# Weight decoding one VectorE operation at a time, and half products for the first batch too

## The chip, the cores and the metric

The kernel runs on one core of a Trainium2 chip. The time of an execution is the device time of that core in microseconds. A profile shows the engines PE (TensorE, the matmuls; PEld is its loading of weights), DVE (VectorE), ACT (ScalarE), POOL (GpSimd) and SP (SyncE, which issues nearly all transfers here). Each engine works through its own queue in program order and waits where an operand or a buffer is not ready.

## The reference

Routed attention with 4 batches, 8 heads, 768 tokens and 64 elements to a head, and after it a feed-forward block on the joined heads.

```python
q_assign = np.argmax(np.einsum('bhsd,hcd->bhsc', q_n, c_n), axis=-1)   # 16 clusters
k_assign = np.argmax(np.einsum('bhsd,hcd->bhsc', k_n, c_n), axis=-1)
mask = q_assign[:, :, :, None] == k_assign[:, :, None, :]
scores = np.where(mask, scale * np.matmul(q, k.transpose(0, 1, 3, 2)), -1e9)
attn = np.exp(scores - np.max(scores, axis=-1, keepdims=True))
attn = attn / (np.sum(attn, axis=-1, keepdims=True) + 1e-09)
x = np.matmul(attn, v)            # joined to 3072 tokens x 512
h = x @ w_in                      # 512 x 2048
g = h * np.clip(h + 3.0, 0.0, 6.0) / 6.0
return (g @ w_out)                # 2048 x 512
```

q, k, v and the result are float32. `w_in` and `w_out` reach the kernel as float64, that is as pairs of 32-bit words, and the kernel builds float32 weights from the two words.

## The kernel before

The attention runs over 16 pairs of heads (4 pairs to a batch), and a pair takes 12 steps: 2 halves of the 384 queries times 6 blocks of 128 keys. The main loop takes two steps at a time, so I call one pass a double step. `n` counts steps (0 to 190, by twos), and `r = n % 12` says where in the pair it is. Batch 0 is n = 0 to 46, batch 1 is n = 48 to 94.

The program is written out by hand in the order in which each engine is to run it (`tc.manual_schedule()`). One double step issues, in this order:

1. `scores` for two steps: PE multiplies q and k (L354), ACT takes the exponential `ex` (L366), and POOL adds the exponentials up in `acc` (L370 and L373; ten additions a pair, none where a half begins; `ex` has four buffers).
2. `attn_v` for the two steps before: PE (L383), and at the end of a half an ACT copy `num` (L389).
3. `in_range`, two ACT passes over the reciprocal of the divide before (L416, L417), and twice in a pair (r = 2 and r = 8) `divide`: PE sums `acc` into `pd` (L404), DVE takes the reciprocal `rcp` (L408) and multiplies it into `xT` (L409).
4. the preparation of the next pair, one part at a time: `turn` (r = 0 and 2), `cluster_scores` (r = 4, PE L291), `route` (r = 6, PE L302 and then DVE `mx` and `one_hot`, L305 and L311), `route_turn` (r = 8 and 10, PE L334).
5. some items of the feed-forward block, as many as `items_by(n + 2)` says.
6. in chosen double steps (`slots`) the decoding of one chunk of weights.

The small PSUM tiles of the parts 3 and 4 come from `scratch`. While `st["early"]` holds (up to `DECODED`), one in three of them is a buffer of its own (`psum_t`, one buffer) and two in three come from `psum_m` (two buffers), which the feed-forward block uses too. So the fourth scratch tile waits for the first, in effect: `route_turn` at r = 10 and `cluster_scores` at r = 4 each wait for the `rcp` of the double step before to have read `pd`.

There are 32 chunks of weights (16 of `w_in`, 16 of `w_out`, 128 x 512 each). `decode_weights(i)` is two ACT passes (L210, L213) and five DVE operations one behind the other: L219, L223, L226, L230 and L233. `load_weights(i + 1)` goes ahead of it; the raw words have two buffers, so that a load waits until the chunk two before has been read. The slots are r = 0, 4, 10 in batch 0 (12 chunks) and r = 0, 2, 4, 6, 10 in batch 1 (20 chunks), the last at n = 94; `DECODED` is 96.

The feed-forward block of batch 0 (`ffn_items`) takes 384 tokens at a time: 16 `up` items (four matmuls of 384 columns, L440, then the gate: ACT L427, DVE L428) and 12 `down` parts (four matmuls of 512 columns, L457), twice. Its first 16 `up` items are spread over n = 52 to 94, and the other 40 items fall to n = 96 to 102. The batches 1 to 3 use `fast_items`: 256 tokens at a time, 8 `up` items (eight matmuls of 256 columns, L504, and after every second one four DVE operations on the gated values, L516) and 7 `down` parts of eight matmuls of 256 columns (L522). The seven parts take the place of eight half-size products: sums and differences of blocks are formed first, as in Strassen's scheme. They need the weight sums `T1` to `T4`, which `weight_sums` forms in eight DVE operations (L493), one in each double step from n = 96.

After the loop's last attention step whatever is left of the feed-forward block runs alone.

Of the kernel before, what the change touches and what calls it, by code (L numbers as in the profile page):

```python
# [8 lines left out]
F32 = mybir.dt.float32  # L9
BF16 = mybir.dt.bfloat16  # L10
U32 = mybir.dt.uint32
I32 = mybir.dt.int32
ALU = mybir.AluOpType
ACT = mybir.ActivationFunctionType
# [4 lines left out]
P = 128  # L19
NCH = S // P  # L20
NC2 = 2 * NCH
HALF = S // 2
NHC = NCH // 2
NG = B * H
NPAIR = NG // 2
DM = 512
DFF = 2048
NKT = DM // P
NFT = DFF // P
WC = 512  # L30
NW = NKT * DFF // WC + NFT
# [85 lines left out]
def fast_path(ctx, tc, ok, q, k, v, centroids, moe_w_in, moe_w_out, out):  # L117
# [3 lines left out]
    nc = tc.nc  # L121
# [15 lines left out]
    yp = pool("yp", 1)  # L137
    decoding = ctx.enter_context(ExitStack())
    rawp = decoding.enter_context(tc.tile_pool(name="rawp", bufs=2))
    decp = decoding.enter_context(tc.tile_pool(name="decp", bufs=2))  # L140
# [3 lines left out]
    psum_m = pool("psum_m", 2, space=PSUM)  # L144
# [54 lines left out]
    def load_weights(i):  # L199
        if i < len(chunks):  # L200
            st["raw", i] = rawp.tile([P, WC, 2], U32, name="raw")
            nc.sync.dma_start(st["raw", i], chunks[i][1])

    def decode_weights(i):
        if not 0 <= i < len(chunks):
            return
        dst, raw = chunks[i][0], st.pop(("raw", i))
        lo, hi = raw[:, :, 0], raw[:, :, 1]
        size = decp.tile([P, WC], BF16, name="wsize")
        nc.scalar.activation(  # L210
            out=size, in_=hi.bitcast(F32), func=ACT.Abs, accum_out=w_totals[:, 0, i : i + 1]
        )
        nc.scalar.activation(  # L213
            out=size, in_=size, func=ACT.Relu, bias=w_low, scale=-1.0,
            accum_out=w_totals[:, 1, i : i + 1],
        )
        top = decp.tile([P, WC], U32, name="wtop")
        unit = decp.tile([P, WC], U32, name="wunit")
        nc.vector.tensor_scalar(  # L219
            out=top, in0=hi, scalar1=3, scalar2=0x3FFFFFFF,  # L220
            op0=ALU.logical_shift_left, op1=ALU.bitwise_and,
        )
        nc.vector.scalar_tensor_tensor(  # L223
            out=top, in0=hi, scalar=0xC0000000, in1=top, op0=ALU.bitwise_and, op1=ALU.bitwise_or
        )
        nc.vector.tensor_scalar(  # L226
            out=unit, in0=top, scalar1=0xFF800000, scalar2=None, op0=ALU.bitwise_and
        )
        top, unit = top.bitcast(F32), unit.bitcast(F32)
        nc.vector.scalar_tensor_tensor(  # L230
            out=unit, in0=lo, scalar=2.0**-52, in1=unit, op0=ALU.mult, op1=ALU.mult
        )
        nc.vector.tensor_tensor(out=dst, in0=top, in1=unit, op=ALU.add)  # L233

# [188 lines left out]
    def gate(g, h):  # L425

        nc.scalar.activation(out=g, in_=h, func=ACT.Relu, bias=half_c, scale=1.0 / 6.0)  # L427
        nc.vector.scalar_tensor_tensor(out=g, in0=g, scalar=1.0, in1=h, op0=ALU.min, op1=ALU.mult)  # L428


    def ffn_items(b):
        slots = g_sb.rearrange("p k i c -> p (k i c)")

        def up(hf, f):
            def item():
                xT = st["xT", b]
                ph = psum_m.tile([P, 512], F32, name="ph", tag="m")
                hh = ph[:, 0:HALF]
                for kt in range(NKT):
                    nc.tensor.matmul(  # L440
                        hh, lhsT=w_in_sb[:, kt, f * P : (f + 1) * P],
                        rhs=xT[:, kt, hf * HALF : (hf + 1) * HALF],
                        start=(kt == 0), stop=(kt == NKT - 1),
                    )
                at = (hf * NFT + f) % 18 * HALF
                st["g", f] = slots[:, at : at + HALF]
                gate(st["g", f], hh)

            return item

        def down(hf, i, part):
            def item():
                if part == 0:
                    st["y"] = psum_m.tile([P, DM], F32, name="py", tag="m")
                py = st["y"]
                for f in range(part * 4, part * 4 + 4):
                    nc.tensor.matmul(  # L457
                        py, lhsT=st["g", f][:, i * P : (i + 1) * P], rhs=w_out_sb[:, f],
                        start=(f == 0), stop=(f == NFT - 1),
                    )  # L460
                if part == 3:
                    y = yp.tile([P, DM], F32, name="y", tag=f"y{i % 2}")
                    nc.vector.tensor_copy(out=y, in_=py)
                    nc.sync.dma_start(out_v[b, hf * NHC + i], y)

            return item

        items = []
        for hf in range(2):
            items += [up(hf, f) for f in range(NFT)]  # L470
            items += [down(hf, i, part) for i in range(NHC) for part in range(4)]
        return items

# [3 lines left out]
    def weight_sums(i):  # L481
        if i == 0:
            decoding.close()
            wtp = pool("wtp", 1)
            for name in ("T1", "T2", "T4"):
                st[name] = wtp.tile([P, HF, HC], F32, name=name)
            st["T3"] = wb[0][1]
        name, a, b = (
            ("T1", wb[0][1], wb[0][0]), ("T2", wb[1][1], st["T1"]), ("T4", wb[1][0], st.get("T2")),
            ("T3", wb[1][1], wb[0][1]),  # L490
        )[i // 2]
        h = slice(i % 2 * HF // 2, (i % 2 + 1) * HF // 2)
        nc.vector.tensor_tensor(out=st[name][:, h], in0=a[:, h], in1=b[:, h], op=ALU.subtract)  # L493


    def fast_items(b):
        def up(m, i):
            def item():
                xT = st["xT", b]
# [72 lines left out]
    def prep_items(g, r):  # L572
# [13 lines left out]
    per_batch = NKT * per_pair  # L586
    total = NPAIR * per_pair
    lag_v, lag_d = 2, 4
    up_half = NFT
    per_ffn = 2 * (NFT + NHC * 4)  # L590
    per_fast = NHC * (HF + 7)

    slots = [
        n for n in range(0, total, 2)
        if n % per_pair in ((0, 4, 10) if n < per_batch else (0, 2, 4, 6, 10))
    ][:NW]
    READY, DECODED = per_batch + lag_d, slots[-1] + 2

    END = 2 * per_batch + NCH + 2

    def items_by(n):

        if n <= DECODED:
            return max(n - READY, 0) * up_half // (DECODED - READY)
        if n <= END:
            return up_half + (n - DECODED) * (per_ffn - up_half) // (END - DECODED)
        return per_ffn + (n - END) * per_fast // per_batch

    st["early"] = True
    fill = []
# [2 lines left out]
    with tc.manual_schedule():  # L615
        nc.scalar.dma_start(cen, centroids.rearrange("h c d -> (h c) d"))
        load(0, "q", "k")
        constants()
        load(0, "v")
        load_weights(0)  # L620
        centroid_norm()
        for part in range(4):
            turn(0, part)
        load(1, "q", "k")
        scores_qk(0)
        scores_qk(1)
        cluster_scores(0)
        route(0)
        for part in range(3):
            route_turn(0, part)  # L630

        for n in range(0, total + lag_d + 2, 2):
            g, r = divmod(n, per_pair)
            for i in (n, n + 1):
                if i < total:
                    scores(i)
            for i in (n - lag_v, n - lag_v + 1):
                if 0 <= i < total:
                    attn_v(i)
            for check in later:  # L640
                check()
            later.clear()
            m = n - lag_d + 1
            if m >= 0 and m % NCH == NCH - 1:
                later.append(divide(m))
            prep = prep_items(g + 1, r)
            if r == 4 and prep:
                prep.pop()()
            if n == DECODED:
                st["early"] = False  # L650
            if m >= 0 and m % per_batch == per_batch - 1:
                fill += (fast_items if m >= per_batch else ffn_items)(m // per_batch)
            if r == 6:
                load(g + 2, "q", "k")
                load(g + 1, "v")
            want = items_by(n + 2) - done if n < total else len(fill)
            want = min(want, len(fill))
            done += want
            for i in range(max(len(prep), want)):
                if i < want:  # L660
                    fill.pop(0)()
                if i < len(prep):
                    prep[i]()
            if n in slots:
                load_weights(slots.index(n) + 1)
                decode_weights(slots.index(n))
            if n >= DECODED and (n - DECODED) // 2 < 8:
                weight_sums((n - DECODED) // 2)
            if n >= total:
                for check in later:  # L670
                    check()
                later.clear()
# [384 lines left out]
```

## Time and profile before

| what | value |
|---|---|
| median of 3 runs | 1089.53 us (1089.1 to 1089.73) |
| the profiled execution | 1088.66 us |
| its span in the trace | 1086.9 us |
| PE busy | 1041.9 us (96%), 5218 matmul records |
| DVE busy | 430.2 us (40%) |
| ACT busy | 396.3 us (36%) |
| POOL busy | 300.9 us (28%) |

A float32 matmul shows as two records in the trace, so L440's 256 records are 128 matmuls. In the page, "busy" is the time in which at least one instruction of the group runs, and a group's mean can be longer than its share of that time, because matmuls overlap at their ends. The 40 slices are 27.2 us each. The first score matmul against the mask (L354 with `xm`) of n = 0, 12, 48, 60, 72, 84 and 96 starts at 15.60, 39.10, 121.45, 162.00, 202.76, 240.63 and 284.54 us; I cut the trace there into pairs.

### The profile page before, as it was taken

How to read it: one execution, taken by the hardware profiler on the slowest of the kernel's cores; microseconds unless marked ns; L12 is line 12 of the kernel's file. 1: busy time of each engine (PE TensorE's matmuls, PEld its weight loads, DVE VectorE, ACT ScalarE, POOL GpSimd, SP SyncE). 2: the span in 40 equal slices, each digit the busy share in tenths (PEclk: the TensorE clock that was granted, in tenths of full speed). 3: DMA queues.
4: the chain of work that ended last, by engine and by line, in shares of the span. 5: the costliest groups of instructions: out<-in, count | busy, mean ns of one | idle time of the engine just before them, and what ended most of it. 6: DMA issues, size and time to landing. Idle time of an engine off the chain costs nothing.

```text
span 1086.9 us, 12783 instructions
## 1 busy us (share of the span) xinstructions
PE 1041.9 (96%) x5218; PEld 672.2 (62%) x5218; DVE 430.2 (40%) x609; ACT 396.3 (36%) x798; POOL 300.9 (28%) x171
## 2 busy tenths in 40 slices
PE   6998979899899999999999999999999999999997
PEld 3443434444445544676667677677667678888886
DVE  4788886799202212331331321332232141413141
ACT  5777857667301301333332442332342330102010
POOL 3766645455100101323231323331322320000000
PEclk9999989999999999999999999999999999999999
DMA  6443244144002000020100202020100000000000
GB/s 155 113 99 101 74 102 122 59 102 121 1 19 54 1 10 20 1 44 21 44 1 1 64 1 44 20 44 1 34 1 1 20 1 1 21 17 4 20 1 24
DMA packets 83540, 42.89 MB, mean 39 GB/s; under 512 B 76304, under 2 KB 76304, under 8 KB 83472
## 3 DMA queue, kind: packets, MB, share of 16 engines
q1 hardware_dynamic: 83328, 41.95, 14.9%
q8 instruction: 43, 0.70, 0.3%
q14 instruction: 25, 0.20, 0.1%
q10 hardware_dynamic: 144, 0.03, 0.0%
HBM read 35.68 MB, written 6.29 MB: 39 GB/s over the span
## 4 chain that ended last, share of the span: by engine, by line
PE 83%; DVE 13%; ACT 2%; issue 1%; POOL 0%; DVEq 0%; POOLq 0%; ACTq 0%
PE ph L504 23%; PE ps L354 12%; PE Y L522 12%; PE pv L383 9%; PE X L522 9%; PE py L457 8%; PE ph L440 6%; DVE rcp L408 3%; DVE wtop L223 2%; DVE wtop L219 2%; PE pqk L278 2%; DVE xT L409 2%; DVE wunit L230 2%; PE pd L404 1%; DVE wunit L226 1%
## 5 line engine op out<-in xcount | busy, mean ns | idle before, releaser
L373 POOL TENSOR_TENSOR acc<-acc,ex 128x768 f32<-128x768 f32 x128 | 239.7, 1873 | 387.2 <-ACT ex L366 381.5
L504 PE MATMUL ph<-xT,w_in_sb 128*128 128x256 f32 x1152 | 259.6, 382 | 0.0
L504 PEld LDWEIGHTS ph<-xT,w_in_sb 128*128 128x128 f32 x1152 | 215.3, 190 | 46.2 <-issue 18.1
L366 ACT ACTIVATE ex<-ps 128x768 f32<-128x768 f32 x192 | 150.2, 806 | 144.5 <-PE ps L354 144.4
L427 ACT ACTIVATE g_sb<-ph,half_c 128x512 f32<-128x512 f32 (+1 forms) x104 | 68.1, 655 | 306.6 <-PE ph L504 245.7
L428 DVE SCALAR_TENSOR_TENSOR g_sb<-g_sb,ph 128x512 f32<-128x512 f32 (+1 forms) x104 | 67.2, 646 | 282.5 <-ACT g_sb L427 282.5
L354 PE MATMUL ps<-xf 64*128 64x384 f32 x768 | 169.4, 520 | 7.2 <-ACT ex L366 7.2
L383 PE MATMUL pv<-ex,vt 128*64 128x384 f32 x768 | 145.3, 499 | 0.0
L370 POOL TENSOR_TENSOR acc<-ex 128x768 f32<-128x768 f32 x32 | 59.0, 1843 | 200.3 <-ACT ex L366 200.3
L408 DVE RECIPROCAL rcp<-pd 128x384 f32<-128x384 f32 x32 | 81.8, 2555 | 76.7 <-PE pd L404 76.7
L354 PEld LDWEIGHTS ps<-xf 64*128 64x128 f32 x768 | 64.8, 190 | 54.5 <-issue 33.0
L383 PEld LDWEIGHTS pv<-ex,vt 128*64 128x64 f32 x768 | 46.7, 136 | 81.2 <-issue 77.9
L440 PE MATMUL ph<-xT,w_in_sb 128*128 128x384 f32 x256 | 87.3, 493 | 2.5 <-DVE g_sb L428 2.5
L457 PE MATMUL py<-w_out_sb,g_sb 128*128 128x512 f32 x192 | 84.0, 594 | 0.0
L440 PEld LDWEIGHTS ph<-xT,w_in_sb 128*128 128x128 f32 x256 | 47.2, 190 | 42.1 <-issue 5.4
L522 PE MATMUL Y<-w_out_sb,g_sb 128*128 128x256 f32 x288 | 66.1, 383 | 0.0
L529 DVE TENSOR_TENSOR y<-y,Y 128x256 f32<-128x256 f32 x36 | 15.1, 420 | 127.2 <-PE Y L522 126.6
L522 PE MATMUL Y<-T,g_sb 128*128 128x256 f32 x288 | 65.3, 380 | 0.0
L522 PE MATMUL X<-w_out_sb,g_sb 128*128 128x256 f32 x288 | 65.3, 380 | 0.0
L354 PE MATMUL ps<-xm 64*128 64x384 bf16 x384 | 64.0, 328 | 0.7 <-ACT xm L338 0.7
L457 PEld LDWEIGHTS py<-w_out_sb,g_sb 128*128 128x128 f32 x192 | 35.9, 190 | 44.2 <-issue 43.3
L522 PEld LDWEIGHTS Y<-w_out_sb,g_sb 128*128 128x128 f32 x288 | 53.9, 190 | 12.9 <-issue 6.0
(88 smaller groups left out, 831.8 us busy)
## 6 DMA issues: line engine op xcount, KB each, us to landing
raw<-in_moe_w_in_dram SPq DMA_DIRECT2D x16, 512.0 KB, 3.6
raw<-in_moe_w_out_dram SPq DMA_DIRECT2D x16, 512.0 KB, 3.6
qk<-in_q_dram SPq DMA_DIRECT2D x32, 192.0 KB, 3.9
qk<-in_k_dram SPq DMA_DIRECT2D x32, 192.0 KB, 4.2
vt<-in_v_dram SPq DMA_DIRECT2D x32, 192.0 KB, 4.2
out_dram<-y SPq DMA_DIRECT2D x24, 256.0 KB, 2.1
cen<-in_centroids_dram ACTq DMA_DIRECT2D x1, 32.0 KB, 1.6
```

What stands on the lines that cost most here:

```text
L354: nc.tensor.matmul(st["ps", n][:, t, 0:HALF], lhsT=x[r, NCH + j], rhs=x[r, hf * NHC : (hf + 1) * NHC], start=first, stop=not first,)
L366: nc.scalar.activation(out=ex, in_=sc, func=ACT.Exp, scale=SM_SCALE)
L370: nc.gpsimd.tensor_tensor(out=acc, in0=st["ex", n - 1], in1=ex, op=ALU.add)
L373: nc.gpsimd.tensor_tensor(out=acc, in0=acc, in1=ex, op=ALU.add)
L383: nc.tensor.matmul(pv[t * D : (t + 1) * D], lhsT=vt[:, j, t], rhs=ex[:, t], start=(j == 0), stop=(j == NCH - 1),)
L408: nc.vector.reciprocal(out=rcp, in_=pd)
L427: nc.scalar.activation(out=g, in_=h, func=ACT.Relu, bias=half_c, scale=1.0 / 6.0)
L428: nc.vector.scalar_tensor_tensor(out=g, in0=g, scalar=1.0, in1=h, op0=ALU.min, op1=ALU.mult)
L440: nc.tensor.matmul(hh, lhsT=w_in_sb[:, kt, f * P : (f + 1) * P], rhs=xT[:, kt, hf * HALF : (hf + 1) * HALF], start=(kt == 0), stop=(kt == ...
L457: nc.tensor.matmul(py, lhsT=st["g", f][:, i * P : (i + 1) * P], rhs=w_out_sb[:, f], start=(f == 0), stop=(f == NFT - 1),)
L504: nc.tensor.matmul(ph[:, t * HC : (t + 1) * HC], lhsT=w_in_sb[:, kt, f * P : (f + 1) * P], rhs=xT[:, kt, 2 * m * P : 2 * (m + 1) * P], sta ...
L522: nc.tensor.matmul(bank[:, half * HC : (half + 1) * HC], lhsT=g_sb[:, kind, i], rhs=w[:, i], start=(first and i == 0), stop=(last and i == ...
```

## The change

`decode_weights` becomes `decoding_steps(i)`, a list of five functions, each with one of the five DVE operations. The first also issues the load of the next chunk and the first ACT pass, the third also the second ACT pass. The loop holds all 160 of them in one list, followed by the eight `weight_sums`, and takes some off its front in every double step: 5, 3, 4, 2, 3 and 4 at r = 0, 2, 4, 6, 8 and 10, which is 21 in a pair and 168 in the eight pairs of batch 0 and 1. The old `ffn_items` goes, and `fast_items` takes its name and serves all four batches. Eight of batch 0's `up` items are spread over n = 52 to 94, 30 items fall to n = 96 to 102, and the last 7 of its 45 come after n = 104.

```diff
-    def decode_weights(i):
...
-        nc.scalar.activation(
-            out=size, in_=hi.bitcast(F32), func=ACT.Abs, accum_out=w_totals[:, 0, i : i + 1]
-        )
-        nc.scalar.activation(
-            out=size, in_=size, func=ACT.Relu, bias=w_low, scale=-1.0,
-            accum_out=w_totals[:, 1, i : i + 1],
-        )
...
+    def decoding_steps(i):
+        got = {}
+        def split():
+            load_weights(i + 1)
+            raw = st.pop(("raw", i))
+            got.update(lo=raw[:, :, 0], hi=raw[:, :, 1])
...
+            nc.scalar.activation(
+                out=got["size"], in_=got["hi"].bitcast(F32), func=ACT.Abs,
+                accum_out=w_totals[:, 0, i : i + 1],
+            )
+            nc.vector.tensor_scalar(
+                out=got["top"], in0=got["hi"], scalar1=3, scalar2=0x3FFFFFFF,
+                op0=ALU.logical_shift_left, op1=ALU.bitwise_and,
+            )
+        def join():
+            nc.vector.scalar_tensor_tensor(
+                out=got["top"], in0=got["hi"], scalar=0xC0000000, in1=got["top"],
+                op0=ALU.bitwise_and, op1=ALU.bitwise_or,
+            )
+        def power():
+            nc.scalar.activation(
+                out=got["size"], in_=got["size"], func=ACT.Relu, bias=w_low, scale=-1.0,
+                accum_out=w_totals[:, 1, i : i + 1],
+            )
+            nc.vector.tensor_scalar(
+                out=got["unit"], in0=got["top"], scalar1=0xFF800000, scalar2=None, op0=ALU.bitwise_and
+            )
+        def rest():
+            unit = got["unit"].bitcast(F32)
+            nc.vector.scalar_tensor_tensor(
+                out=unit, in0=got["lo"], scalar=2.0**-52, in1=unit, op0=ALU.mult, op1=ALU.mult
+            )
+        def total():
+            nc.vector.tensor_tensor(
+                out=chunks[i][0], in0=got["top"].bitcast(F32), in1=got["unit"].bitcast(F32), op=ALU.add
+            )
+        return [split, join, power, rest, total]
...
-    def ffn_items(b):
-        slots = g_sb.rearrange("p k i c -> p (k i c)")
...
-    def fast_items(b):
+    def ffn_items(b):
...
-    up_half = NFT
-    per_ffn = 2 * (NFT + NHC * 4)
-    per_fast = NHC * (HF + 7)
-    slots = [
-        n for n in range(0, total, 2)
-        if n % per_pair in ((0, 4, 10) if n < per_batch else (0, 2, 4, 6, 10))
-    ][:NW]
-    READY, DECODED = per_batch + lag_d, slots[-1] + 2
+    up_first = NFT // 2
+    per_ffn = NHC * (NFT // 2 + 7)
+    decode = [step for i in range(NW) for step in decoding_steps(i)]
+    decode += [lambda i=i: weight_sums(i) for i in range(8)]
+    share = {0: 5, 2: 3, 4: 4, 6: 2, 8: 3, 10: 4}
+    READY, DECODED = per_batch + lag_d, 2 * per_batch
     END = 2 * per_batch + NCH + 2
+    up_last = per_ffn - 7
     def items_by(n):
         if n <= DECODED:
-            return max(n - READY, 0) * up_half // (DECODED - READY)
+            return max(n - READY, 0) * up_first // (DECODED - READY)
         if n <= END:
-            return up_half + (n - DECODED) * (per_ffn - up_half) // (END - DECODED)
-        return per_ffn + (n - END) * per_fast // per_batch
+            return up_first + (n - DECODED) * (up_last - up_first) // (END - DECODED)
+        return up_last + (n - END) * per_ffn // per_batch
...
-                fill += (fast_items if m >= per_batch else ffn_items)(m // per_batch)
+                fill += ffn_items(m // per_batch)
...
-            if n in slots:
-                load_weights(slots.index(n) + 1)
-                decode_weights(slots.index(n))
-            if n >= DECODED and (n - DECODED) // 2 < 8:
-                weight_sums((n - DECODED) // 2)
+            for step in decode[: share[r]]:
+                step()
+            del decode[: share[r]]
```

More of the change, by code (lines that the diff above doesn't have):

```diff
@@ L202, in load_weights @@
             nc.sync.dma_start(st["raw", i], chunks[i][1])
-    def decode_weights(i):
[L205 to L209, printed above, removed]
-        nc.scalar.activation(
-            out=size, in_=hi.bitcast(F32), func=ACT.Abs, accum_out=w_totals[:, 0, i : i + 1]
-        )
-        nc.scalar.activation(
-            out=size, in_=size, func=ACT.Relu, bias=w_low, scale=-1.0,
-            accum_out=w_totals[:, 1, i : i + 1],
-        )
[L217 to L233, printed above, removed]
@@ new lines, in decoding_steps @@
+    def decoding_steps(i):
[4 more added lines that the diff above has]
+            got.update(lo=raw[:, :, 0], hi=raw[:, :, 1])
+            got["size"] = decp.tile([P, WC], BF16, name="wsize")
+            got["top"] = decp.tile([P, WC], U32, name="wtop")
+            got["unit"] = decp.tile([P, WC], U32, name="wunit")
+            nc.scalar.activation(
[29 more added lines that the diff above has]
+        return [split, join, power, rest, total]
@@ L428, in gate @@
         nc.vector.scalar_tensor_tensor(out=g, in0=g, scalar=1.0, in1=h, op0=ALU.min, op1=ALU.mult)
-    def ffn_items(b):
-        slots = g_sb.rearrange("p k i c -> p (k i c)")
[L434 to L472, printed above, removed]
     HF, HC = NFT // 2, DM // 2
```

## The prediction

> **What bounds the kernel now.** I read the page's slices first, then the windows of the pairs, then the groups of instructions, then the timeline at two places.
>
> ```profile
> PE   6998979899899999999999999999999999999997
> DVE  4788886799202212331331321332232141413141
> ```
>
> PE is the bound from the twelfth slice on. Before it PE has gaps, and there DVE is the busiest of the others. The cut into pairs (columns: stretch, length, then busy time of PE, PEld, DVE, ACT, POOL, granted clock, DMA share) shows how much:
>
> ```profile
> 15.60:39.10 23.50, 23.50 (x148) 10.74 (x149) 11.90 (x14) 17.49 (x37) 16.95 (x10) 0.93 0.39 101
> 39.10:66.56 27.46, 24.80 (x166) 11.05 (x164) 24.41 (x24) 21.00 (x46) 18.87 (x11) 1.00 0.42 102
> 121.45:162.00 40.55, 32.54 (x182) 15.10 (x180) 36.31 (x40) 26.69 (x62) 20.03 (x11) 0.92 0.36 95
> 162.00:202.76 40.76, 38.29 (x206) 18.52 (x203) 26.11 (x32) 26.08 (x59) 20.46 (x11) 1.00 0.34 94
> 240.63:284.54 43.91, 39.61 (x206) 19.25 (x203) 32.32 (x38) 27.90 (x65) 19.32 (x10) 0.96 0.30 75
> 284.54:1086.90 802.36, 791.17 (x3760) 553.77 (x3756) 211.08 (x364) 204.41 (x376) 145.26 (x80) 1.00 0.07 18
> ```
>
> A pair of batch 0 without its start is 24.8 us of PE work in 27.46 us (three pairs alike). Batch 1 (121.45 to 284.54) takes 163.1 us, and PE is busy for 146.1 us of it. What follows has 11.2 us of PE gaps, 7.4 of them after the last matmul (at 1079.4 us).
>
> The cause of the gaps is a resource that DVE and POOL can't use together:
>
> ```profile
> 43.64 0.42 DVE L219 TENSOR_SCALAR wtop<-raw 128x512 uint32<-128x512 uint32 x1
> 44.10 2.26 DVE L223 SCALAR_TENSOR_TENSOR wtop<-raw,wtop 128x512 uint32<-128x512 uint32 x1
> 43.99 1.81 POOL L370 TENSOR_TENSOR acc<-ex 128x768 f32<-128x768 f32 x1 [3.19 <-ACT ex L366]
> 154.77 0.80 PE L334 MATMUL po<-ident_q,one_hot 128*128 128x128 bf16 x6 [6.24 <-DVE rcp L408]
> ```
>
> L223 takes 0.69 us where POOL is idle. Here it starts 0.11 us behind a POOL addition and ends 0.56 us after that ends: it stood still for all of it. Every decode operation shows such cases (maxima of 1.9 to 2.3 us against 0.42 to 0.69), and so does L409; the reciprocal, L305 and L311, which read PSUM, never do. The last line is the worst wait: a lump of five decode operations, two of them held up by POOL, stood ahead of `rcp` in DVE's queue, and PE waited 6.24 us for the scratch tile that `rcp` frees.
>
> **The change part by part.** PE work first.
>
> ```profile
> L504 PE MATMUL ph<-xT,w_in_sb 128*128 128x256 f32 x1152 | 259.6, 382 | 0.0
> L440 PE MATMUL ph<-xT,w_in_sb 128*128 128x384 f32 x256 | 87.3, 493 | 2.5 <-DVE g_sb L428 2.5
> L457 PE MATMUL py<-w_out_sb,g_sb 128*128 128x512 f32 x192 | 84.0, 594 | 0.0
> L522 PE MATMUL Y<-w_out_sb,g_sb 128*128 128x256 f32 x288 | 66.1, 383 | 0.0
> L522 PE MATMUL Y<-T,g_sb 128*128 128x256 f32 x288 | 65.3, 380 | 0.0
> L522 PE MATMUL X<-w_out_sb,g_sb 128*128 128x256 f32 x288 | 65.3, 380 | 0.0
> L522 PE MATMUL X<-T,g_sb 128*128 128x256 f32 x144 | 33.1, 383 | 0.0
> ```
>
> Batch 0 loses L440 and L457, 87.3 + 84.0 = 171.3 us. It gains a third of what the other three batches spend: 259.6 / 3 + (66.1 + 65.3 + 65.3 + 33.1) / 3 = 86.5 + 76.6 = 163.1 us. PE saves 8.2 us, nearly all of it in the `down` parts. An `up` item was 87.3 / 32 = 2.73 us and becomes 86.5 / 24 = 3.60 us.
>
> Where this work lies moves too. Batch 1 held 16 old `up` items (43.7 us) and will hold 8 new ones (28.8 us). The PE-bound stretch after it goes from 171.3 - 43.7 = 127.6 to 163.1 - 28.8 = 134.3 us: **+6.7 us**. Its gaps I leave as they are: the interleaving there is that of today's batches 1 to 3. DVE gains some 19 us, most of it there (24 gates of 0.69 for 32 of 0.55, 48 operations L516 of 0.42, 15 additions L529 of 0.42, less 6 copies L463 of 0.69). PE hides it, DVE being busy for 211 of 802 us there; were that cover gone, 19 us would be the price.
>
> Decoding. The 160 operations stay, but batch 0 gets 21 in a pair instead of 15, and batch 1 gets 21 (13 and the eight sums in its last pair) instead of 25. One decode operation holds the resource for its own time less the 0.13 us by which L223 overlapped: the five own times 0.42, 0.69, 0.43, 0.69, 0.69 give 2.27 us, 0.454 each. L409 (0.56 alone) holds it for 0.43. POOL holds it for 10 x 1.81 = 18.1 us in a pair. So a pair of batch 0 needs 18.1 + 15 x 0.454 + 0.86 = 25.8 us of it today, and the pair took 27.46: it is 94% occupied, and that, not PE's 24.8, sets the pace. After the change the need is 18.1 + 21 x 0.454 + 0.86 = 28.5 us, at 94% **30.3 us**. DVE's own queue agrees: own times 21 x 0.584 + 2 x 0.56 + 2 x 2.56 (`rcp`) + 1.25 (`mx`, `one_hot`) = 19.8 us, and of POOL's 18.1 us only some 6.4 can fall beside `rcp`, `mx` and `one_hot`, which makes 19.8 + 11.7 = 31.5, less 23 overlaps of 0.13, 28.5 again. Bounds for such a pair: PE's 24.8 if POOL's additions all fall where DVE needs nothing, and 32.8 if each group of a double step meets POOL as today's do (DVE waited 24.4 - 16.3 = 8.1 us over 5 groups, three lumps and two L409; 8 groups make 13.0, on top of 19.8). I take 30.3, as the need and the queue agree. The first pair has an empty queue to fill and took 23.5; I give it 26 of its 28.5. Batch 0: 26 + 3 x 30.3 = 116.9 against 105.85: **+11.0 us**.
>
> The Trainium skill ("SBUF — State Buffer", the section on the two sides) says that the second engine is blocked for the first one's whole instruction. By that the need would be 18.1 + 21 x 0.584 + 1.12 = 31.5 us a pair, 33.5 at 94%, and batch 0 would cost 9.6 us more in its last three pairs; L223 above shows that 0.13 us of each is free.
>
> Batch 1 after: PE needs 24.8 a pair and 1, 2, 2 and 3 `up` items, 28.4, 32.0, 32.0, 35.6. The resource needs 28.5, then with four operations L516 (0.42 - 0.13 each) 29.7 twice, and in the last pair 18.1 + 13 x 0.454 + 0.86 + 6 x 0.29 + 8 x 1.09 (a sum L493 takes 1.22) = 35.3; at 94% 30.3, 31.5, 31.5, 37.5. Where PE and the resource are as near as in the two middle pairs I add to PE's need the 2.3 us that the pair at 162.00 (40.76 - 38.29) and the next one (37.87 - 35.67) lose today. 30.3 + 34.3 + 34.3 + 37.5 = 136.4, and 2 us for matmuls on a lower clock after a gap (the 0.92 and 0.96 above): 138.4 against 163.1, **-24.7 us**. That is where single operations pay: at most five, mostly three or four, stand ahead of `rcp`, and the waits of 6.24 and (at 265 us) 4.3 us should shrink.
>
> The sums now come before n = 96, where the first `down` parts read them; the last four are issued at n = 94 and DVE may be late: **+1 us**, between 0 and the 4 x 1.22 + 2 x 1.81 = 8.5 us of that double step. Loads: SP issues the same 32, each waiting for L230 of the chunk two before; between that and the next first operation lie six decode operations, 8.3 us at 21 in 29 us, and a load lands in 3.6 us. ACT's first pass stood 2.0 us on a load once; I count nothing, and 2.0 for each of 32 chunks at worst, were that cover gone. What would then be late is `ex`, queued behind it on ACT, and PE's next scores.
>
> **Sum.** +11.0 - 24.7 + 6.7 + 1 = -6.0 us on the span of 1086.9: 1080.9. The execution lay 1.8 us above its span (1088.66), and the median 0.9 above that: **1083.5 us**.
>
> **The rivals.**
>
> *PE is the bound throughout.* If POOL's four buffers of `ex` let its additions slide beside the reciprocals, DVE's queue never lags. Batch 0, with 0.5 us a pair of gaps left: 23.5 + 3 x 25.3 = 99.4 (-6.5). Batch 1: PE's 128.0 and 3 us of gaps (-32.1). With +6.7: -31.9, 1057.6 us. For it: `ex` has four buffers, and the steps without decoding run at PE's pace today. Against: 25.8 of 27.46 us already taken.
>
> *The queue ahead of `rcp` becomes a standing wait.* Five operations at r = 0 and four at r = 10 lie between one `rcp` and the next; `cluster_scores` at r = 4 waits for it, and so does ACT's L416, behind which `ex` stands. Then pairs go at the upper bound, 32.8 instead of 30.3, 2.5 us more in each of the eight pairs, and the sums are late by 1 us more: -6.0 + 20.0 + 1.0 = +15.0, 1104.5 us. It decides from 6.0 / 8 = 0.75 us on, that is from pairs of about 31.1 us in batch 0. For it: 6.24 us lost this way today, and 1 us in a pair counts eight times. Against: today's lumps put the same five at r = 0, and 30.3 has a 6% loss in it already.
>
> *The saving is just given back.* Pairs of 31.0 us, 0.7 more in each of eight: -6.0 + 5.6 = -0.4, 1089.1 us. It lies between the forecast and the rival above, with the same for and against.
>
> **How the numbers follow.** The forecast has 0.53, the PE-bound rival 0.13, the standing wait 0.25, the last 0.09. A change of 0.2% (2.2 us) is about what this kernel's measurement can tell. Faster is 0.53 + 0.13 = 0.66, the same 0.09, slower 0.25. The forecast's own range is 1075 to 1087, pairs 1.0 us shorter to 0.45 us longer. For 8 in 10 it reaches over some of the fast rival and half of the slow one: 1066 to 1098.
>
> **What would show it.** Pairs of batch 0 of 29.3 to 30.8 us with DVE busy nearly throughout; batch 1 under 142 us with no PE wait on `rcp` over 4 us; some 163 us in the matmuls of batch 0's block; the stretch from n = 96 on near 809 us. Pairs of 25 us or of 33 us would prove the forecast wrong, and so would ACT's first pass waiting for loads many times.

## The result and the profile after

| | before | after |
|---|---|---|
| median of the runs | 1089.32 us (4 runs) | 1093.97 us (4 runs, 1091.98 to 1096.17) |
| ratio, 95% interval | | 1.0044 (1.002 to 1.0069) |
| the profiled execution, its span | 1088.66, 1086.9 us | 1096.17, 1094.4 us |
| mean granted TensorE clock | 0.993 | 0.983 |

The change made the kernel about 0.4% slower, a small loss but clear of noise. The forecast was 0.55% faster. The profiled execution is the slowest of the four, so its span shows 7.5 us of loss where the medians show 4.7.

The page's sums and slices of the changed kernel:

```profile
PE 1042.7 (95%) x5490; PEld 729.0 (67%) x5490; DVE 510.2 (47%) x658; ACT 395.2 (36%) x796; POOL 309.8 (28%) x171
PE   6888879998999999999999999999999999999997
DVE  5899999989724150252242153143145131413141
```

PE is as busy as before (1041.9 us) though its work fell, and its idle time in the span rose from 45.0 to 51.7 us. DVE is busy for nine tenths or more in most of the first ten slices.

The windows of the pairs, cut as before where the first score matmul against the mask starts (length, busy PE, PEld, DVE, ACT, POOL, granted clock, DMA share):

```profile
16.88:39.60 22.72, 22.72 (x147) 10.46 (x149) 17.00 (x18) 20.67 (x48) 17.58 (x9) 0.96 0.48 122
39.60:75.14 35.54, 27.53 (x165) 12.24 (x163) 34.74 (x30) 23.18 (x54) 21.60 (x12) 0.90 0.36 93
103.68:133.11 29.43, 24.97 (x165) 11.08 (x163) 28.78 (x28) 21.95 (x50) 18.35 (x10) 1.00 0.42 112
133.11:172.18 39.07, 31.48 (x182) 15.34 (x180) 36.77 (x37) 25.29 (x58) 20.93 (x12) 0.91 0.38 98
172.18:205.00 32.82, 31.79 (x198) 17.17 (x196) 30.38 (x30) 23.41 (x53) 19.34 (x11) 1.00 0.39 101
241.31:281.58 40.27, 36.88 (x213) 21.35 (x211) 38.37 (x41) 23.16 (x51) 23.15 (x12) 0.96 0.22 56
281.58:1094.40 812.82, 799.02 (x4032) 606.63 (x4028) 259.05 (x400) 208.30 (x381) 149.67 (x80) 0.99 0.07 18
```

Pairs without a long stall take 23 to 33 us. Pairs with one take 35 to 40 us, at a granted clock of 0.90 to 0.96. One such stall, in the timeline of DVE, POOL and PE (start, duration, instruction, idle time before it in brackets):

```profile
55.54 1.92 DVE L235 TENSOR_SCALAR wunit<-wtop 128x512 uint32<-128x512 uint32 x1
57.49 2.19 DVE L241 SCALAR_TENSOR_TENSOR wunit<-raw,wunit 128x512 f32<-128x512 uint32 x1
59.72 2.19 DVE L246 TENSOR_TENSOR w_in_sb<-wtop,wunit 128x512 f32<-128x512 f32 x1
61.83 2.03 DVE L219 TENSOR_SCALAR wtop<-raw 128x512 uint32<-128x512 uint32 x1
63.90 2.17 DVE L225 SCALAR_TENSOR_TENSOR wtop<-raw,wtop 128x512 uint32<-128x512 uint32 x1
...
59.10 2.27 POOL L387 TENSOR_TENSOR acc<-ex 128x768 f32<-128x768 f32 x1
61.44 4.08 POOL L390 TENSOR_TENSOR acc<-acc,ex 128x768 f32<-128x768 f32 x2
...
67.44 0.82 PE L351 MATMUL po<-ident_q,one_hot 128*128 128x128 bf16 x6 [4.76 <-DVE one_hot L328]
68.41 1.65 PE L371 MATMUL ps<-xf 64*128 64x384 f32 x4
...
74.39 0.92 PE L371 MATMUL ps<-xf 64*128 64x384 f32 x4
```

As long as POOL has an addition ready, DVE gets one decode operation through for each addition: five in a row take 2 us apiece instead of 0.42 to 0.69. `mx` and `one_hot` stand behind them, and PE waits 4.76 us. After that wait the same four score matmuls take 1.65 us instead of 0.92, until some 6 us later; the granted clock is 0.58 from 68.4 to 74.4 us. In the whole trace 53 of the 160 decode operations took over 1.2 us (33 before), and all of them together 175.9 us (144.5 before).

A second kind of wait is ACT's on a load, at which `ex` stands in the queue:

```profile
49.43 0.67 ACT L215 ACTIVATE wsize<-raw 128x512 bf16<-128x512 f32 x1 [4.81 <-DMA raw<-in_moe_w_in_dram]
50.94 0.92 PE L371 MATMUL ps<-xf 64*128 64x384 f32 x4 [3.25 <-ACT ex L383]
```

There were six of these waits on loads, 12.2 us in all (one of 2.0 us before).

### The profile page after: what moved, and what is told of

The parts are those of the page before. It is cut to its first block, busy times and chain, and to the rows that moved or that the text cites. A ratio compares the mean times of both kernels' runs of the same rounds, so it can differ in the third digit from the quotient of the medians.

```text
span 1094.4 us, 13387 instructions
## 1 busy us (share of the span) xinstructions
PE 1042.7 (95%) x5490; PEld 729.0 (67%) x5490; DVE 510.2 (47%) x658; ACT 395.2 (36%) x796; POOL 309.8 (28%) x171
## 4 chain that ended last, share of the span: by engine, by line
PE 80%; DVE 16%; ACT 2%; issue 1%; DMA 0%; POOL 0%; DVEq 0%; POOLq 0%; SPq 0%; ACTq 0%
PE ph L477 30%; PE Y L495 15%; PE ps L371 11%; PE X L495 11%; PE pv L400 8%; DVE rcp L425 3%; DVE wtop L219 2%; DVE wunit L241 2%; DVE g_sb L489 2%; DVE wtop L225 2%; DVE wunit L235 2%; PE pqk L295 1%; PE pd L421 1%; DVE w_out_sb L246 1%; DVE w_in_sb L246 1%
## 5 line engine op out<-in xcount | busy, mean ns | idle before, releaser
L477 PE MATMUL ph<-xT,w_in_sb 128*128 128x256 f32 x1536 | 345.5, 383 | 3.4 <-DVE rcp L425 3.4
L477 PEld LDWEIGHTS ph<-xT,w_in_sb 128*128 128x128 f32 x1536 | 289.0, 191 | 60.3 <-issue 13.2
L371 PE MATMUL ps<-xf 64*128 64x384 f32 x768 | 173.9, 532 | 10.5 <-ACT ex L383 10.5
L445 DVE SCALAR_TENSOR_TENSOR g_sb<-g_sb,ph 128x512 f32<-128x512 f32 x96 | 66.0, 688 | 239.1 <-ACT g_sb L444 239.1
L444 ACT ACTIVATE g_sb<-ph,half_c 128x512 f32<-128x512 f32 x96 | 66.0, 687 | 296.6 <-PE ph L477 296.6
L489 DVE TENSOR_TENSOR g_sb<-g_sb 128x256 f32<-128x256 f32 x192 | 108.6, 607 | 3.3
L495 PE MATMUL Y<-w_out_sb,g_sb 128*128 128x256 f32 x384 | 88.0, 382 | 0.0
L495 PE MATMUL X<-w_out_sb,g_sb 128*128 128x256 f32 x384 | 87.7, 381 | 0.0
L495 PEld LDWEIGHTS X<-w_out_sb,g_sb 128*128 128x128 f32 x384 | 72.1, 190 | 14.2 <-issue 3.0
L495 PEld LDWEIGHTS Y<-T,g_sb 128*128 128x128 f32 x384 | 72.1, 190 | 9.3
L297 ACT COPY xf<-pqk 128x384 f32<-128x384 f32 x64 | 29.1, 481 | 48.4 <-PE pqk L295 48.4
```

Source lines behind the costliest of these rows:

```text
L297: nc.scalar.copy(out=dst, in_=pt)
L371: nc.tensor.matmul(st["ps", n][:, t, 0:HALF], lhsT=x[r, NCH + j], rhs=x[r, hf * NHC : (hf + 1) * NHC], start=first, stop=not first,)
L477: nc.tensor.matmul(ph[:, t * HC : (t + 1) * HC], lhsT=w_in_sb[:, kt, f * P : (f + 1) * P], rhs=xT[:, kt, 2 * m * P : 2 * (m + 1) * P], sta ...
L489: nc.vector.tensor_tensor(out=out_, in0=in0, in1=in1, op=op)
L495: nc.tensor.matmul(bank[:, half * HC : (half + 1) * HC], lhsT=g_sb[:, kind, i], rhs=w[:, i], start=(first and i == 0), stop=(last and i == ...
```

## The experiments

Stages are cut at n = 0, 48 and 96 in each profiled execution. The stretch before n = 0 (15.5 to 17.0 us) does the same work in all of them. Each ratio is to runs of the kernel before on the same chip, whose median lay between 1088.7 and 1090.4 us.

| kernel | median us | ratio to before (95%) | batch 0 | batch 1 | from n = 96 |
|---|---|---|---|---|---|
| before | 1089.3 | | 105.8 | 163.1 | 802.3 |
| changed | 1094.0 | 1.0044 (1.002 to 1.0069) | 116.2 | 148.5 | 812.8 |
| half products alone | 1101.3 | 1.0106 (1.0091 to 1.0122) | 105.9 | 160.4 | 817.4 |
| spreading alone | 1087.6 | 0.9983 (0.9974 to 0.9992) | 115.8 | 151.1 | 802.5 |
| changed, three raw buffers | 1110.1 | 1.0184 (1.017 to 1.0198) | 124.8 | 153.1 | 812.7 |
| changed, without additions | 1051.2 | 0.9646 (0.9628 to 0.9664) | 98.3 | 128.7 | 805.2 |
| spreading, without additions | 1059.6 | 0.9716 (0.9695 to 0.9738) | 96.0 | 143.1 | 802.3 |
| spreading, 8 up items fewer in batch 1 | 1094.7 | 1.0043 (1.0027 to 1.006) | 116.1 | 135.0 | 822.9 |
| spreading, 13 and 27 a pair | 1091.2 | 1.0021 (1.0003 to 1.0039) | 107.0 | 162.4 | 802.3 |
| the same, additions on DVE | 1065.7 | 0.977 (0.9753 to 0.9787) | 97.2 | 149.2 | 802.3 |
| half products, additions on DVE | 1068.5 | 0.9801 (0.9784 to 0.9818) | 96.0 | 140.3 | 812.5 |
| the same, all items by n = 104 | 1064.9 | 0.977 (0.9751 to 0.9789) | 96.6 | 140.4 | 809.4 |
| changed, sums as ACT copies | 1094.2 | 1.005 (1.003 to 1.007) | 116.1 | 148.3 | 814.3 |
| changed, all items by n = 104 | 1092.1 | 1.0018 (1.0008 to 1.0027) | 118.1 | 149.0 | 807.9 |

**Half products alone.** Decoding in the old lumps, the sums behind the last chunk.

```diff
-            for step in decode[: share[r]]:
-                step()
-            del decode[: share[r]]
+            if n in slots:
+                load_weights(slots.index(n) + 1)
+                decode_weights(slots.index(n))
+            if n == slots[-1]:
+                for i in range(8):
+                    weight_sums(i)
```

> Half products for batch 0 as in the changed kernel, but the decoding in lumps of five operations in the old slots, and the eight weight sums right behind the last chunk at n = 94. Theory L (DVE's queue, held up by POOL's lock, sets the pace of batches 0 and 1, and spreading the decoding moved 6 operations a pair into the batch that has the least PE work): batch 0 stays at 106 us as before, batch 1 loses the 14.9 us of up items that moved out and goes from 163 to about 148 us, the stretch from n = 96 grows by 7 to 12 us; median 1079 to 1085 us, faster than both. Rival G (the saving of PE is eaten by lower clock and new waits whatever the decoding does): batch 1 near 155 us and a median of 1088 to 1093 us.

Batch 0 was as before, but batch 1 fell by only 2.7 us and the median rose to 1101.3 us: theory L missed by some 20 us, and even the rival was too hopeful. So of the two edits it is the half products, with the new places of the items and the sums that come with them, that cost time here. Spreading, added to them, saves 1101.3 - 1094.0 = 7.3 us.

**Spreading alone.** The old `ffn_items`, with the sums from n = 96 on.

```diff
-    decode += [lambda i=i: weight_sums(i) for i in range(8)]
...
+            if n >= DECODED and (n - DECODED) // 2 < 8:
+                weight_sums((n - DECODED) // 2)
```

> The decoding in single operations spread as in the changed kernel, but batch 0's feed-forward block as before (384 tokens, no half products) and the weight sums from n = 96 on as before. Theory L: batch 0 takes 116 us as in the changed kernel (106 before), batch 1 with its 16 old up items stays near 163 us, so the median is about 1099 us (1095 to 1103), slower than before. Rival G: spreading costs nothing by itself and the median is 1086 to 1091 us.

Theory L had batch 0 right (115.8) and batch 1 wrong (151.1 instead of 163). The median is in rival G's range, but not for its reason, as spreading does cost time in batch 0. It costs 10 us there and gives back 12 in batch 1; the sum, 0.17% faster, is at the edge of what can be told.

**Three buffers for the raw words.**

```diff
-    rawp = decoding.enter_context(tc.tile_pool(name="rawp", bufs=2))
+    rawp = decoding.enter_context(tc.tile_pool(name="rawp", bufs=3))
...
-            load_weights(i + 1)
+            load_weights(i + 2)
```

> The changed kernel with three buffers of raw words instead of two and each load issued two chunks ahead. Theory W (ACT's first pass of a chunk waits for its load, because with two buffers the load can only start when DVE has read the chunk two before, and ex stands behind that pass): the 12.2 us of ACT waits on loads go, PE's longest wait on ex (3.25 us) goes, and the median falls by 5 to 10 us to about 1086 us. Theory L: the loads only pass on DVE's lag; ACT then runs into other waits, and the median falls by at most 3 us, to 1091 to 1094 us.

Both theories missed: ACT's waits on loads went (none above 0.1 us is left), and the kernel became 16 us slower. In this kernel's timeline ACT now stands on `xT` instead, and PE on DVE's queue:

```profile
91.42 0.52 ACT L433 ACTIVATE rcp<-rcp 128x384 f32<-128x384 f32 x1 [8.53 <-DVE xT L426]
93.20 0.90 PE L319 MATMUL pr<-ident,cs 128*128 128x128 f32 x3 [5.69 <-DVE w_in_sb L246]
95.42 1.65 PE L371 MATMUL ps<-xf 64*128 64x384 f32 x4 [1.32 <-ACT ex L383]
```

DVE had needed 16 us for ten decode operations ahead of that `rcp` and `xT`. The waits on loads came with DVE's lag: in the kernel without additions, below, one of 0.5 us is left with two buffers as well. That they also held POOL back, so that DVE caught up sooner, would explain the loss, but it is argued, not shown.

**Without POOL's additions.** The denominators are sums of two blocks only.

```diff
-        elif j > 1:
-            acc = st["acc", g, hf]
-            nc.gpsimd.tensor_tensor(out=acc, in0=acc, in1=ex, op=ALU.add)
```

> The changed kernel without POOL's additions past the first of each half: 2 of 10 in a pair are left, and the denominators are sums of two blocks only. Theory L: DVE's decode operations take 0.42 to 0.69 us nearly throughout, the pairs of batch 0 fall to 24.5 to 26 us, PE's waits on rcp and one_hot go, batch 1 falls to about 130 us, and the time is 1060 to 1068 us. Theory W: the waits of ACT on loads stay, pairs of batch 0 stay at 28 us or more, and the time is over 1082 us.

1051.2 us: faster even than theory L's range. Three pairs in the windows of this kernel, two of them from batch 1:

```profile
41.48:66.06 24.58, 24.58 (x166) 11.05 (x164) 20.97 (x29) 21.92 (x50) 3.74 (x2) 1.00 0.55 135
115.22:143.34 28.12, 28.12 (x181) 14.09 (x179) 23.07 (x33) 22.99 (x52) 3.62 (x2) 1.00 0.53 133
208.78:243.91 35.13, 35.13 (x213) 20.17 (x211) 24.78 (x38) 23.71 (x53) 3.62 (x2) 1.00 0.24 64
```

PE has no gap in any of them, at full clock, with the same decoding in the same places and more transfers per microsecond. So POOL's additions, and not the decode operations or the loads as such, make the stalls.

> The spread-only kernel without POOL's additions past the first of each half (denominators are sums of two blocks), to be held against the changed kernel without them (1051.2 us), which has half products for batch 0 as well. Theory M (the half products save PE's 8 us, but only show it where batch 1 is bound by PE; with POOL's additions batch 1 is bound by DVE and POOL, and the up items that moved out of it had been free there): without the additions batch 1 takes PE's own 143 to 145 us and the time is 1058 to 1062 us, 7 to 10 us above 1051.2. Rival G (half products cost batch 0's block more than they save, wherever it lies): 1051 us or less.

The same removal on the spreading-alone kernel gave 1059.6 us, as theory M said. Between these two kernels the half products save 1059.55 - 1051.24 = 8.3 us: what PE's rows promise. With the additions they cost 1094.0 - 1087.6 = 6.4 us.

**Eight up items fewer in batch 1**, on the spreading-alone kernel.

```diff
-    up_half = NFT
+    up_half = NFT // 2
```

> The spread-only kernel with 8 instead of 16 of batch 0's old up items in batch 1; the other 8, 21.8 us of PE work, come after n = 96. No half products, the same work in all. Theory M: batch 1 falls from 151 us by 8 us at most, the stretch from n = 96 grows by 21 to 22 us, and the median goes from 1087.6 to 1100 us or more. Rival B (batch 1 is bound by PE, as the prediction's sum took it): batch 1 falls by 18 to 22 us and the median stays within 4 us of 1087.6.

Neither expectation holds. Batch 1 fell by 151.1 - 135.0 = 16.2 us of the 21.8, so PE's work does count there, and theory M in its plain form (batch 1 has room for nothing but free work) falls. The median rose by 7.1 us.

**Additions on DVE in batches 0 and 1**, one double step late, with 13 operations a pair in batch 0 and 27 in batch 1 (29 with half products).

```diff
+        if n < 2 * per_batch:
+            adds.append((n, add_up))
+        else:
+            add_up(nc.gpsimd)
...
+            while adds and adds[0][0] < n:
+                adds.pop(0)[1](nc.vector)
...
+            share = shares[n >= per_batch]
```

> The spread-only kernel with the additions of batches 0 and 1 on DVE instead of POOL, one double step late, and 13 decode operations a pair in batch 0, 27 in batch 1; POOL adds from n = 96 on. Nothing is left for DVE to wait for on POOL, but DVE's own work grows by ten operations of 0.96 us a pair. Theory L (the lock is the cost): DVE needs 15.1 + 9.6 = 24.7 us of a pair in batch 0 and some 35 us in batch 1, near PE's 24.8 and 35.7; batch 0 takes 100 to 104 us, batch 1 148 to 156 us, and the median is 1068 to 1080 us. Rival D (DVE's load counts as such, whoever shares its port): pairs of 28 and 41 us and a median of 1086 us or more.

1065.7 us, 2.3% faster than before, just below theory L's range. Two of its pairs:

```profile
38.95:63.53 24.58, 24.58 (x165) 11.06 (x163) 23.29 (x31) 20.66 (x47) 0.00 (x0) 1.00 0.44 114
147.44:186.81 39.37, 38.33 (x205) 18.52 (x203) 31.89 (x47) 26.52 (x61) 0.00 (x0) 1.00 0.37 97
```

DVE does POOL's ten additions as well, 79 of the 80 in 0.95 to 0.97 us, against 1.81 on POOL. The one exception, 2.59 us, fell behind n = 96 beside an addition of POOL. In the first of these pairs it is still busy for less time than the 24.41 us of the same pair before, with 13 decode operations instead of 15, because nothing holds it up.

> The changed kernel with the additions of batches 0 and 1 on DVE in the same way, and 13 operations of the list a pair in batch 0, 29 in batch 1. DVE needs 37 us of a pair in batch 1 (29 operations with eight sums of 1.22 among them, ten additions, gates and their sums), PE 32. Theory M: batch 1 stays bound by DVE at 148 to 154 us, the half products gain nothing, the stretch from n = 96 is 3 to 5 us longer, and the median is 0 to 8 us above that of the kernel with additions on DVE and no half products. Rival: with the lock gone the half products pay and the median is 5 to 9 us below it.

Theory M had the median right, 1068.5 us, 2.8 above the last (the intervals of the two ratios just overlap), but not the reason. Batch 1 did not stay at 148 to 154 us: it fell by 8.8 us to 140.3. The stretch from n = 96 took 10.2 us more, not 3 to 5.

> The spread-only kernel with 13 decode operations a pair in batch 0 and 27 in batch 1, and POOL's additions left on POOL: the kernel with additions on DVE (1065.7 us) less that move, to tell its two edits apart. Theory L: the port that DVE and POOL share needs 18.1 + 13 x 0.454 + 0.9 = 24.9 us of a pair in batch 0 and 31.2 in batch 1; batch 0 takes 102 to 107 us, batch 1 155 to 168 us, and the median is 1084 to 1095 us, so that the gain of 22 us is the additions' move. Rival S (the gain came from the other shares): 1070 us or less.

This control has the same shares and the additions left on POOL: 1091.2 us, as theory L said. The gain of 25 us (27 by the ratios to before) is the additions' move. Was it POOL's hold on DVE, or only that POOL is slow? In the changed kernel's trace PE's waits on POOL itself come to 0.4 us in all; its waits of over 3 us are on DVE, whose operations are three to five times as long beside POOL, or on ACT where ACT itself had stood on a load (3.25 us at 50.94) or on DVE's `xT` (3.79 us at 140.29).

**The sums as ACT copies** (the differences of the weights are left out).

```diff
-        nc.vector.tensor_tensor(out=st[name][:, h], in0=a[:, h], in1=b[:, h], op=ALU.subtract)
+        nc.scalar.copy(out=st[name][:, h], in_=a[:, h])
```

> The changed kernel with each of the eight weight sums in batch 1 replaced by an ACT copy of its first operand (the differences of the weights are left out), so that DVE's list ends after 160 operations. It takes 8 x 1.22 = 9.8 us of DVE's work, all needing the port that POOL shares, out of the last pair of batch 1. Theory M (the half products' own DVE work is what batch 1 can't hide): the last pair falls from 40.3 us to PE's 35.1 to 37 us, batch 1 by 4 to 7 us, and the median by as much, to 1087 to 1090 us; the rest of batch 1's loss is the additions on gated values and the lag built up before. Rival Q (batch 1's loss is single stalls of DVE's queue and the lower clock behind them, wherever the work lies): the last pair stays over 39 us and the median at 1092 to 1095 us.

Rival Q: the last pair took 41.9 us, not less, and the median did not move. The trace agrees: in the last pair of both kernels the longest wait of PE is one of 3.4 us, on an `rcp` that runs before the first sum. The sums are not what costs in this kernel.

**All of batch 0's items by n = 104.**

```diff
-    up_last = per_ffn - 7
+    up_last = per_ffn
```

> The changed kernel with all 45 items of batch 0's block by n = 104 instead of 38, so that batches 1 to 3 fall on the same double steps as in the kernel before. The work is the same. Theory P (behind n = 104 the changed kernel puts an odd up item with its four DVE additions on the double step before the reciprocal at r = 8, where POOL's additions block them and PE waits for rcp; that is why n = 104 to 190 takes 465.1 us with POOL's additions and 457.6 without): the stretch from n = 104 falls to about 459 us, the median by 4 to 7 us, to 1087 to 1090 us. Rival: the stretch stays at 464 us or more and the median at 1092 to 1095 us.

> The same shift (all 45 items by n = 104) on the kernel with half products and the additions of batches 0 and 1 on DVE (1068.5 us). Theory P: its stretch from n = 104 falls from 463.5 to about 459 us and the median to 1062 to 1065 us, which would be the fastest with the reference's output. Rival: 1067 us or more.

In both kernels the steps from n = 104 to the last attention step take 458.8 us again, from 465.1 and 463.5: theory P has the place right. In the changed kernel the whole stretch from n = 96 shrank by 4.9 us, but the median by only 1.9, which is in the rival's range. With additions on DVE it fell by 3.6 to 1064.9 us, which with the 1065.7 above is the fastest of the kernels that leave nothing out. What happens at n = 104 in the changed kernel's timeline:

```profile
402.88 4.80 DVE L489 TENSOR_TENSOR g_sb<-g_sb 128x256 f32<-128x256 f32 x4
403.46 3.94 POOL L390 TENSOR_TENSOR acc<-acc,ex 128x768 f32<-128x768 f32 x2 [28.86 <-ACT ex L383]
410.20 0.38 PE L351 MATMUL po<-ident_q,one_hot 128*128 128x128 bf16 x4 [1.25 <-DVE rcp L425]
411.74 1.65 PE L371 MATMUL ps<-xf 64*128 64x384 f32 x4
```

The four additions on gated values take 4.80 us against POOL instead of 4 x 0.42 = 1.7, `rcp` stands behind them, PE waits, and its granted clock falls from 1.00 to 0.50 (411.70 to 413.50 us).

## Why the prediction was wrong, point by point

- *PE saves 8.2 us*: right. The matmuls of all four blocks, by their groups in the changed kernel, come to 652.2 us, 163.1 for one:

```profile
L477 PE MATMUL ph<-xT,w_in_sb 128*128 128x256 f32 x1536 | 345.5, 383 | 3.4 <-DVE rcp L425 3.4
L495 PE MATMUL Y<-w_out_sb,g_sb 128*128 128x256 f32 x384 | 88.0, 382 | 0.0
L495 PE MATMUL X<-w_out_sb,g_sb 128*128 128x256 f32 x384 | 87.7, 381 | 0.0
L495 PE MATMUL Y<-T,g_sb 128*128 128x256 f32 x384 | 87.0, 380 | 0.0
L495 PE MATMUL X<-T,g_sb 128*128 128x256 f32 x192 | 44.0, 382 | 0.0
L371 PE MATMUL ps<-xf 64*128 64x384 f32 x768 | 173.9, 532 | 10.5 <-ACT ex L383 10.5
L400 PE MATMUL pv<-ex,vt 128*64 128x384 f32 x768 | 147.7, 506 | 0.0
```

  The last two rows, the attention's own work, took 169.4 and 145.3 us before: the saving went into matmuls on a lower clock behind stalls.
- *Batch 0, +11.0 us*: right in size, +10.4, and the five kernels with the same 21 operations, two raw buffers and POOL's additions agree (115.8 to 118.1 us). But the sum fits the total and not the single pairs: 22.7, 35.5, 28.5 and 29.4, for 26 and three times 30.3. Nor does its rule carry over: with 13 operations a pair the need is 24.9 us, 26.5 at 94%, and the pairs after the first took 25.4, 29.2 and 30.1. So part of the agreement is luck.
- *Batch 1, -24.7 us*: this is the term that failed; it was -14.6. I had put the four pairs at 30.3, 34.3, 34.3 and 37.5 us, plus 2 us of lower clock; they took 39.1, 32.8, 36.3 and 40.3. Without additions PE needs 126.8 us there, about the 128.0 of the sum. On top came 14.8 us of gaps where the sum allowed 8.4, and 133.7 - 126.8 = 6.9 us of slower matmuls where it allowed 2. The step that failed is the one from "at most five, mostly three or four, stand ahead of `rcp`" to shorter waits. The count was right, but an operation that meets POOL takes some 2 us. I read from the traces how long each `rcp` starts after the last matmul of its `pd`. For the eight of batch 1 that is 24.1 us in all before (the longest 7.5) and 26.5 in the changed kernel (the longest 8.9, below), but 5.9 with spreading alone: there the waits did shrink, and the half products undid it.

```profile
250.42 1.55 DVE L489 TENSOR_TENSOR g_sb<-g_sb 128x256 f32<-128x256 f32 x4
251.89 2.04 DVE L235 TENSOR_SCALAR wunit<-wtop 128x512 uint32<-128x512 uint32 x1
251.65 8.41 POOL L390 TENSOR_TENSOR acc<-acc,ex 128x768 f32<-128x768 f32 x4 [2.87 <-ACT ex L383]
260.98 2.55 DVE L425 RECIPROCAL rcp<-pd 128x384 f32<-128x384 f32 x1
263.58 5.41 PE L477 MATMUL ph<-xT,w_in_sb 128*128 128x256 f32 x16 [3.39 <-DVE rcp L425]
```

  A need divided by 94% is a throughput. It says nothing of DVE's lag coming due at once, which stops PE for 2 to 5 us and may then lower its clock for as long again. The first pair of batch 1 shows it best: PE had 3.6 us of block work in it, and it took 39.1 us; in the spread kernels with the same shares, two raw buffers and POOL's additions it took 37.9 to 41.3 us, and 28.1 and 29.9 without additions. A smaller slip: the need of the last pair counts six additions on gated values where the program issues eight, 0.6 us.
- *+6.7 us from n = 96, its gaps as they are*: the first part was too high (+2.9 without POOL's additions), the second wrong: PE's gaps there rose from 11.1 to 13.8 us, and its matmuls grew longer at a lower clock. The stretch grew by 10.5 us. The 19 us of DVE work that I let PE hide is not hidden where L489 meets POOL ahead of `rcp`.
- *Sums, +1 us*: no wait of PE on them shows, and taking them off DVE changed nothing.
- *Loads, nothing*: wrong in the trace (12.2 us of ACT waits), but removing these waits made the time worse, and without additions all but 0.5 us of them went. With two buffers they come and go with DVE's lag.
- *The standing wait*: the rival with 0.25 had the mechanism (DVE's queue ahead of `rcp`, and as it turned out ahead of `one_hot`) and the direction. Its form, 2.5 us in every pair, was not what happened, nor did it decide in batch 0.

Open: with half products, batch 1 gave back 2.7 us for the 14.9 us of PE work that left it, with old items 16.2 for 21.8. Against the kernel with eight old items the changed one takes 148.5 - 135.0 = 13.5 us more in batch 1, and 28.8 - 21.8 = 7.0 of these are the new items' own PE work; the cause of the rest stays open. The sums are not the reason. The additions on gated values (16 in batch 1) are left as a candidate and were not tried alone. Their own time is small: 12 of the 16 ran before the cut at n = 96, four together in 1.7 us, none held up by POOL. But their place may count: in the lines of the last pair above, four of them ran just before POOL began on four additions, and four of the five decode operations behind them then met POOL. The changed kernel's four times lie at 1092 and at 1096 us; only one execution was profiled, so what makes that difference is not shown.

## What to carry to other kernels

If two engines exclude each other, add their times for the resource before spreading work over them, and look at what stands behind the blocked engine in its queue: in the changed kernel 53 instead of 33 decode operations met the other engine, and with spreading alone 46. An engine that is twice as fast at the same operation may take over the slower one's work at a profit, even when it is the busier of the two: moving 80 additions from POOL to DVE was worth 25 us, where the edit under study cost 5. And saved work on the bound engine counts in full only where that engine has no gaps: without POOL's additions the 8 us were gained, with them they were lost, and with the additions on DVE 0.8 us of them showed at best (1065.7 to 1064.9).

## What the runs showed of the hardware

- POOL with several additions ready and DVE with several operations that POOL holds up take turns, one for one: the five decode operations from 55.54 to 66.07 us, beside five additions, took 10.5 us where they need 2.9.
- A gap need not be long to lower the clock: two waits of 1.25 and 0.67 us, 0.4 us of matmuls between them, were followed by matmuls at 1.65 us (411.74, granted clock 0.50), while one gap of 3.25 us (50.94) was followed by matmuls at the full 0.92 (granted clock 1.00).
